# Window attention with a SwiGLU gate in float32: the split weights in six tiles of half a unit in place of three of a whole one

## The chip, the core and the metric

The kernel runs on one core of a Trainium2 chip. The metric is the device time of one launch in microseconds (us); of three runs of the kernel before, the median is 863.67 us (863.49 to 864.08). Five engines work side by side, each through its own instructions in order: TensorE (PE in the profile, PEld for its weight loads), VectorE (DVE), ScalarE (ACT), GpSimd (POOL) and SyncE (SP), which here issues nearly all of the DMA transfers. They wait for each other by semaphores.

## What is computed

```python
x = A_x                                   # 2048 tokens x 512
xn = _layernorm(x, axis=-1)
qkv = xn @ wqkv                           # 32 heads of 16
scores = einsum("bhqd,bhkd->bhqk", q, k) * (Dh ** -0.5)   # the 256 keys up to the query
s = (softmax(scores) @ v) @ wo
f = (silu(xn @ w_gate) * (xn @ w_up)) @ w_down            # 512 -> 1792 -> 512
return x + s * silu(f)
```

## The kernel before

The products with weights are made in parts: every weight and every activation is split into a high part (rounded to `float32r`) and a low part (the rest), and high times high, low times high and high times low are summed. The array of TensorE is used as two halves of 64 rows each, called half 0 and half 1 here, which work at the same time on different products; each product needs both halves, one after the other, and its PSUM bank is handed from one half to the other by a small VectorE copy (`ho`).

The tokens go in four chunks of 512. The dense work is a list of 120 **units** in an order that is fixed when the program is built: `Proj` (q and k of two groups of heads, PSUM tiles `a`), `Values` (`vp`), `GateUp` (gate `g` and up `u` of 128 hidden columns), `Down` (`d`) and `Wo` (`s`). A unit has two **items** (the last `Wo` has four), and an item fills one PSUM bank. In `Proj` and `GateUp` (class `Stationary`) item 0 reads only the first 512 columns of the unit's weights and item 1 only the second 512. In `Values`, `Down` and `Wo` (class `Moving`) the items are tokens, and each reads all of the unit's weights.

Between the dense matmuls stands the attention, in 32 units of four heads, numbered in the names: for unit 7 the products `b7_...` (for the row maxima, read by VectorE as `jk`), then `c7_...` (scores, turned into `p` by an ACT exponential, then masked by POOL), then `pv7_...`. The `b` and `c` products share four PSUM banks (`pr0` to `pr3`), so a new one can only begin when ACT or DVE has read an old one.

**Weights.** Unit j's weights are fetched by one SP DMA into a raw tile `wr` of 128x1024 (two such buffers, one more for j = 2). The split is two ACT copies that make `wh` (line 413) and two POOL subtractions that make `wl` (line 418), 512 columns each. `wh` and `wl` are tiles of 128x1024 in three buffers each, so unit j takes those of unit j-3. `w_split` (line 399) queues the four instructions when the raw tile has landed and unit j-3 has wholly ended (`item_end`, line 441), and the fetch of unit j+2 is queued half a microsecond ahead of the end of both low halves (line 426). A unit's first item may start when all of its weights are split (line 1360).

**Order.** All of this is laid out when the program is built: a planner keeps a model of each engine's clock, and from it decides which half takes which matmul next (`choice`, `next_mm`), and in which order ACT, POOL, DVE and SP get their instructions (`do`, `dma`, `pump`: among those ready the one with the smallest ready time plus slack). What comes out is one fixed list per engine; on the chip each engine works through its list and waits by semaphores where it has to. So a change of the planner's rules changes all of the lists. Each of SP's DMAs takes one of eight semaphores in turn, and so can only be issued when the one eight issues ahead of it has landed.

Of the kernel before, what the change touches and what calls it, by code (L numbers as in the profile page):

```python
# [10 lines left out]
F32R = mybir.dt.float32r  # L11
BF16 = mybir.dt.bfloat16
AF = mybir.ActivationFunctionType
ALU = mybir.AluOpType
# [3 lines left out]
P = 128  # L18
# [6 lines left out]
KC = D // P  # L25
# [29 lines left out]
def tile_window_attention_swiglu_gate(  # L55
# [10 lines left out]
    nc = tc.nc  # L66
    ctx.enter_context(tc.manual_schedule())
    pers = ctx.enter_context(tc.tile_pool(name="pers", bufs=1))
# [14 lines left out]
    def sb(name, shape, dtype, kind, n):  # L83
        return pers.tile(shape, dtype, name=name, tag=ring(kind, n), bufs=1)

    def f32(ap):
        return ap.bitcast(F32)
# [18 lines left out]
    def do(e, ready, cost, fn, then=None, slack=0.5, can=None, lat=None):  # L106
        seq[0] += 1
        queue[e].append((ready + slack, seq[0], ready, cost, fn, then, can, LAT.get(e, 0.0) if lat is None else lat))
# [16 lines left out]
    def timer(t, fn, *a):  # L125
        seq[0] += 1
        heapq.heappush(timers, (t, seq[0], fn, a))
# [41 lines left out]
    fb_free = {f"pf{i}": 0.0 for i in range(NF)}  # L169
    rb_free = {f"pr{i}": 0.0 for i in range(NR)}  # L170

    def bank_time(pool, n=1):
        t = sorted(v for v in pool.values() if v is not None)
        return t[n - 1] if len(t) >= n else None
# [49 lines left out]
    normed = {}  # L224
# [85 lines left out]
    xhigh = {}  # L310
    xlow = {}
# [42 lines left out]
    def half(r):  # L354
        return slice(R * r, R * r + R)

    def latest(times):
        times = list(times)
        return None if any(t is None for t in times) else max(times)

    class Unit:
        src = None
        width = 0

        def wts(self, r):
            return wtile[self.n]


        def inputs(self, i):
            return 0.0  # L370

    wtile = {}
    wready = {}
    landed = {}
    ended_unit = {}

    def w_fetch(j):
        u = weighted.get(j)
# [16 lines left out]

    raw = {}
    wpart = {}

    def w_split(j):
        if j not in landed or (j >= 3 and j - 3 not in ended_unit):  # L400
            return
        t = max(landed.pop(j), ended_unit.get(j - 3, 0.0))
        w = weighted[j].width
        hi, lo = [], []
        cuts = [(a, min(a + 512, w)) for a in range(0, w, 512)]
        left = [len(cuts)]

        def high(a, b):
            if not hi:
                hi.append(sb(f"wh{j}", [P, 1024], F32R, "wh", 3))  # L410
                lo.append(sb(f"wl{j}", [P, 1024], F32R, "wl", 3))
                wtile[j] = [hi[0], lo[0]]
            nc.scalar.activation(hi[0][:, a:b], raw[j][:, a:b], AF.Copy)  # L413

        def low(a, b):
            if j == 0 and a == 0:
                nc.gpsimd.tensor_copy(spare, xt[0, list(normed)[-1][1]][:, :1])
            nc.gpsimd.tensor_tensor(lo[0][:, a:b], raw[j][:, a:b], f32(hi[0][:, a:b]), op=ALU.subtract)  # L418

        def done(t, a):  # L420
            wpart[j, a, 1] = t
            left[0] -= 1
            if left[0] == 0:
                wready[j] = t
                if j:
                    timer(t - 0.5, w_fetch, j + 2)

        def after_high(t, a, b, sl):
            wpart[j, a, 0] = t
            do("G", t, 0.17 + 0.0021 * (b - a), lambda: low(a, b), lambda t: done(t, a), sl, lambda: len(normed) >= 4)  # L430

        for n, (a, b) in enumerate(cuts):
            sl = (0.0 if j >= 3 else 0.2) + 0.3 * n
            if j == 0:
                sl = -3.0 + 0.1 * n
            do("S", t, 0.13 + 0.00078 * (b - a), lambda a=a, b=b: high(a, b),
               lambda t, a=a, b=b, sl=sl: after_high(t, a, b, sl), sl)

    item_ended = {}

    def item_end(j, t):
        item_ended[j] = item_ended.get(j, 0) + 1
        if item_ended[j] == 2 * weighted[j].items:
            ended_unit[j] = t
            w_split(j + 3)

    def handover(pb):
        nc.vector.tensor_copy(pers.tile([MW, 1], F32, name="ho", tag=ring("ho", 2), bufs=1), pb[:MW, 0:1])  # L448
# [1 line left out]
    def mm(pb, a, b, first, last):  # L450
        return nc.tensor.matmul(pb, a, b, start=first, stop=last, skip_group_check=True)  # L451
# [43 lines left out]
    class Stationary(Unit):  # L495

        width = 1024
        items = 2

        def inputs(self, i):
            if self.c == 0 and self.n == 0:
# [1 line left out]
            return latest(xready.get((self.c, k)) for k in range(KC))  # L505

        def mms(self, i, r, pb):
            w = [t.rearrange("p (a k n) -> p a k n", a=2, k=KC) for t in self.wts(r)]
            xs = xn[self.c % 2]
            if self.c == 0 and self.n == 0 and i == r:  # L510
                for a, b in ((0, 0), (1, 0), (0, 1)):
                    for part in range(2):
                        n = slice(256 * part, 256 * part + 256)
                        for k in range(KC):
                            def go(first, last, k=k, a=a, b=b, n=n):
                                return mm(pb[:, n], w[a][half(r), i, k, :], xs[b][half(r), k, n], first, last)
                            yield 256, go, lambda k=k, a=a, b=b, part=part: latest(
                                [(xlow if b else xhigh).get((k, part)), wpart.get((0, 512 * i, a))]
                            )
                return  # L520
            for k in range(KC):
                for a, b in PAIRS:
                    def go(first, last, k=k, a=a, b=b):
                        return mm(pb, w[a][half(r), i, k, :], xs[b][half(r), k, :], first, last)
                    yield 512, go

    class Proj(Stationary):
# [107 lines left out]
    class Moving(Unit):  # L635
# [2 lines left out]
        items = 2  # L638

        def mms(self, i, r, pb):  # L640
            w = [t[:, : self.width].rearrange("p (k n) -> p k n", n=256) for t in self.wts(r)]
            per = 4 // self.items
            for t in range(per):
                tok = slice((per * i + t) * P, (per * i + t + 1) * P)
                for k in range(self.width // 256):
                    for a, b in PAIRS:
                        def go(first, last, t=t, k=k, a=a, b=b, tok=tok):
                            mm(
                                pb[:, t * 256 : t * 256 + 256], self.act(k, a)[half(r), tok],
                                w[b][half(r), k, :], first, last,  # L650
                            )
                        yield 256, go

# [626 lines left out]
    weighted = {}  # L1280
# [30 lines left out]
    def next_mm(r):  # L1311
        if extra[r]:
            cols, go, then = extra[r].pop(0)
            go()
            issue(r, cols)
            if then:
                then(clock[r] + 0.25)
            return
        if run[r] is None:
            n, opens = choice(r)  # L1320
            u, i = stream[n]
            if opens:
                opened[0] += 1
                banks[n], tags[n] = bank(fb_free, u.name(i))
                if isinstance(u, Wo):
                    u.begin(i)
            else:
                half_done[r].remove(n)
            run[r] = [list(u.mms(i, r, banks[n])), 0, n, opens]
        todo, m, n, opens = run[r]  # L1330
        u, i = stream[n]
        cols, go = todo[m][:2]
        go(opens and m == 0, not opens and m == len(todo) - 1)
        issue(r, cols)
        if r == 0:
            work[0] += cols * MM / 512
        run[r][1] += 1
        if run[r][1] < len(todo):
            return
        run[r] = None  # L1340
        t = clock[r] + 0.2
        item_end(u.n, t)
        if opens:
            pb = banks[n]
            half_done[1 - r].append(n)
            do("V", t, 0.1, lambda: handover(pb), lambda t: handed.__setitem__(n, t), -1.0)
        else:
            closed[0] += 1
            tag = tags.pop(n)
            u.done(i, banks.pop(n), t, lambda t: fb_free.__setitem__(tag, t))  # L1350

    def choice(r):
        t = max(clock[r], now[0])
        for n in half_done[r]:
            if handed.get(n, 1e9) <= t:
                return n, False
        n = opened[0]
        if n < len(stream):
            u, i = stream[n]
            w = wpart.get((0, 512 * i, 0)) if u.n == 0 else wready.get(u.n)  # L1360
            w = latest([bank_time(fb_free), u.inputs(i), w])
            if w is not None and w <= t:
                return n, True
        return None
# [28 lines left out]
    while True:  # L1393
        now[0] = max(front[0], min(clock))
        while marks and marks[-1][0] <= work[0] / PACE - LEAD:
            _, fn, a = marks.pop()
# [11 lines left out]
        done = False  # L1408
        if not any(extra):
            s = work[0] / PACE - LEAD  # L1410
            for st in sorted(streams, key=lambda st: st[-1][0] if st else 1e9):
                if not st:
                    continue
                due, need, fn, a = st[-1]
# [4 lines left out]
                t = need(*a)  # L1419
                if t is not None and t <= now[0]:  # L1420
# [4 lines left out]
                    done = True  # L1425
# [4 lines left out]
        if able:  # L1430
            idle = 0
            r = min(able, key=lambda r: clock[r])
# [45 lines left out]
```

## Time and profile before

| | |
|---|---|
| median of 3 runs | 863.67 us |
| the profiled execution, its own time | 865.33 us |
| span of its trace | 863.6 us |
| PE matmuls busy | 854.2 us (99%) |
| POOL, ACT, DVE busy | 595.9, 495.7, 486.2 us |
| the 240 ACT copies `wh` | 136.4 us, 616 ns mean |
| the 240 POOL subtractions `wl` | 296.7 us, 1259 ns mean |
| HBM read and written | 107.74 and 29.62 MB, 159 GB/s over the span |

Times in the views are counted from the start of the span. A row of the timeline gives start, duration, engine, line, operation, output<-inputs, shape and count, and in brackets the idle time of the engine ahead of it with what ended it. A row of SP is the issue of a DMA, not its transfer. Matmuls are pipelined: their starts say more than their durations, whose ends are modelled.

### The profile page before, as it was taken

The page shows a single profiled execution, that of the slowest core. Times are in us where ns is not written, and L with a number is a line of the kernel's source. Part 1 is how long each engine was busy: PE and PEld are TensorE (multiplying, and loading weights), DVE is VectorE, ACT ScalarE, POOL GpSimd, SP SyncE. Part 2 cuts the span into 40 slices and gives each one's busy share as a digit, 9 for nine tenths or more (in the row PEclk, how much of TensorE's full clock was granted, in tenths as well). Part 3 has the DMA queues.
Part 4 walks back from the last instruction along what each step waited for, and adds up shares of the span by engine and source line. Part 5 has one row for each costly group of instructions (what it writes and reads, how often), then busy time and mean ns, then how long its engine had stood idle before and what let it go on. Part 6 is the DMA issues. An engine that isn't in the chain of part 4 may idle for free.

```text
span 863.6 us, 29615 instructions
## 1 busy us (share of the span) xinstructions
PE 854.2 (99%) x11960; PEld 785.1 (91%) x11960; DVE 486.2 (56%) x1633; ACT 495.7 (57%) x1056; POOL 595.9 (69%) x630
## 2 busy tenths in 40 slices
PE   9999999999999999999999999999999999999997
PEld 8999999899799898999799999999999989889897
DVE  4364566555566555656565656566556656645234
ACT  4355555546665566565677566655656665656532
POOL 7555566658776775666879586666668697869764
PEclk9999999999999999999999999999999999999999
DMA  5764645455756963464777866455556668553241
GB/s 176 198 179 132 195 112 172 142 156 153 195 154 183 275 171 111 96 181 123 174 201 185 223 183 192 108 174 136 165 135 174 176 188 223 166 147 113 87 149 62
DMA packets 67628, 139.58 MB, mean 162 GB/s; under 512 B 12690, under 2 KB 21394, under 8 KB 67492
## 3 DMA queue, kind: packets, MB, share of 16 engines
q1 hardware_dynamic: 67204, 137.17, 57.3%
q8 instruction: 94, 1.54, 0.8%
q10 hardware_dynamic: 288, 0.52, 0.2%
q14 instruction: 42, 0.34, 0.2%
HBM read 107.74 MB, written 29.62 MB: 159 GB/s over the span
## 4 chain that ended last, share of the span: by engine, by line
PE 94%; DMA 3%; DVE 1%; ACT 1%; issue 0%; SPq 0%; POOL 0%; DVEq 0%; POOLq 0%; ACTq 0%
PE u L451 18%; PE d L451 18%; PE g L451 18%; PE a L451 11%; PE pv L1152 8%; PE c L1115 5%; PE s L451 5%; PE vp L451 5%; PE b L961 5%; DMA r<-rd 1%; DMA wr<-wgu 1%; DVE jk L969 0%; DMA xt<-x 0%; PE xp L469 0%; ACT wh L413 0%
## 5 line engine op out<-in xcount | busy, mean ns | idle before, releaser
L418 POOL TENSOR_TENSOR wl<-wr,wh 128x512 fp32r<-128x512 f32 x240 | 296.7, 1259 | 166.0 <-ACT wh L413 146.9
L969 DVE CUSTOM_DVE_ANT_0 jk<-b,maskb 128x384 bf16<-128x384 f32 (+2 forms) x512 | 271.7, 531 | 152.1 <-PE b L961 87.4
L1076 ACT ACTIVATE p<-c 128x384 f32<-128x384 f32 (+1 forms) x480 | 206.8, 496 | 87.1 <-PE c L1115 78.5
L451 PE MATMUL d<-wh,hh 64*128 64x256 f32 x1792 | 236.7, 278 | 0.0
L451 PEld LDWEIGHTS d<-wh,hh 64*128 64x128 f32 x1792 | 208.7, 185 | 1.4 <-issue 0.8
L451 PE MATMUL d<-wl,hh 64*128 64x256 f32 x896 | 191.7, 279 | 0.0
L413 ACT ACTIVATE wh<-wr 128x512 fp32r<-128x512 f32 x240 | 136.4, 616 | 69.1 <-issue 15.6
L451 PE MATMUL g<-xh,wh 64*128 64x512 f32 x448 | 173.3, 395 | 0.0
L451 PE MATMUL g<-xl,wh 64*128 64x512 f32 x448 | 172.9, 395 | 0.0
L451 PE MATMUL g<-xh,wl 64*128 64x512 f32 x448 | 172.6, 394 | 0.0
L451 PE MATMUL u<-xh,wh 64*128 64x512 f32 x448 | 172.2, 395 | 0.0
L451 PE MATMUL u<-xl,wh 64*128 64x512 f32 x448 | 171.6, 395 | 0.0
L451 PE MATMUL u<-xh,wl 64*128 64x512 f32 x448 | 171.4, 395 | 0.0
L451 PEld LDWEIGHTS d<-wl,hh 64*128 64x128 f32 x896 | 143.1, 185 | 0.4
L961 PE MATMUL b<-k,q 48*128 48x384 f32 (+1 forms) x512 | 113.3, 339 | 2.0 <-ACT p L1076 2.0
L1089 POOL TENSOR_SCALAR_AFFINE_SELECT p<-p 128x512 f32<-128x512 f32 x128 | 81.1, 637 | 48.9 <-ACT p L1076 44.3
L1115 PE MATMUL c<-q,k 49*128 49x384 f32 (+1 forms) x704 | 106.2, 305 | 0.7 <-ACT p L1076 0.7
L451 PE MATMUL a<-xh,wh 64*128 64x512 f32 (+1 forms) x264 | 88.6, 396 | 0.2 <-DVE ho L448 0.2
L451 PE MATMUL a<-xl,wh 64*128 64x512 f32 (+1 forms) x264 | 87.5, 387 | 0.0
L451 PE MATMUL a<-xh,wl 64*128 64x512 f32 (+1 forms) x264 | 86.8, 386 | 0.0
L451 PEld LDWEIGHTS g<-xh,wl 64*128 64x128 f32 x448 | 82.3, 186 | 3.0
L451 PEld LDWEIGHTS g<-xl,wh 64*128 64x128 f32 x448 | 82.0, 185 | 3.1 <-issue 0.2
(102 smaller groups left out, 2039.6 us busy)
## 6 DMA issues: line engine op xcount, KB each, us to landing
wr<-wgu SPq DMA_DIRECT2D x56, 512.0 KB
k<-qkd SPq DMA_DIRECT2D x48, 192.0 KB
wr<-wqk SPq DMA_DIRECT2D x16, 512.0 KB
qkd<-qkh SPq DMA_DIRECT2D x32, 256.0 KB
qkd<-qkl SPq DMA_DIRECT2D x32, 256.0 KB
q<-qkd SPq DMA_DIRECT2D x64, 128.0 KB
wr<-wdn SPq DMA_DIRECT2D x16, 512.0 KB
od<-ev SPq DMA_DIRECT2D x32, 256.0 KB
```

The source lines that it names most:

```text
L413: nc.scalar.activation(hi[0][:, a:b], raw[j][:, a:b], AF.Copy)
L418: nc.gpsimd.tensor_tensor(lo[0][:, a:b], raw[j][:, a:b], f32(hi[0][:, a:b]), op=ALU.subtract)
L451: return nc.tensor.matmul(pb, a, b, start=first, stop=last, skip_group_check=True)
L961: nc.tensor.matmul(pb[:, :w], qs[u % 3][r : r + 48, p, qb * P : (qb + 1) * P], ks[u % 3][r : r + 48, p, lo : lo + w], start=True, stop=True,)
L969: nc.vector.tensor_tensor_reduce(junk[:, :n], pb[:, :n], maskb[:, 3 * P - n :], 1.0, -3.0e38, ALU.add, ALU.max, m[:, col : col + 1],)
L1076: nc.scalar.activation(t[:, h, :], pc[:, a:b], AF.Exp, scale=DH ** -0.5)
L1089: nc.gpsimd.affine_select(s, s, [[0, 4], [1, P]], ALU.is_ge, 0.0, base=0, channel_multiplier=-1)
L1115: nc.tensor.matmul(pc[:, at0 : at0 + w], ks[u % 3][r : r + 49, p, k0 : k0 + P], qs[u % 3][r : r + 49, p, qb * P : qb * P + w], start=(i == ...
L1152: nc.tensor.matmul(pbs[r][0][32 * j : 32 * j + 32, q0:q1], vt[half(r), (4 * c + kb) % VT, VW * (4 * g + j) : VW * (4 * g + j) + 32], t[hal ...
```

## The change

`wh` and `wl` become tiles of 128x512, six tags each, of which half a of unit j takes number (2j + a) mod 6: the same memory, the same buffers, in halves. Each half has its own conditions: it is split when the raw tile has landed and the same half of unit j-3 is free (`w_cut`), and a half is free when all items that read it have ended on both halves of the array (`uses`: item a alone for `Stationary`, all items for `Moving`; `item_end`). An item of a `Stationary` unit needs only its own half to start (`need`); a `Moving` one needs both. The fetch of unit j+2 is still queued when both low halves are done. The numbers of instructions, their shapes and the bytes moved stay.

```diff
-        def wts(self, r):
-            return wtile[self.n]
+        def wts(self, a):
+            return wtile[self.n, a]
+        def uses(self, a):
+            return range(self.items)
+        def need(self, i):
+            return latest(wready.get((self.n, a)) for a in range(2))
...
     def w_split(j):
-        if j not in landed or (j >= 3 and j - 3 not in ended_unit):
+        for a in range(2):
+            w_cut(j, a)
+
+    def w_cut(j, a):
+        old = divmod(2 * j + a - NW, 2)
+        if j not in landed or (j, a) in wtile or (old[0] >= 0 and old not in wfreed):
             return
-        t = max(landed.pop(j), ended_unit.get(j - 3, 0.0))
...
-                hi.append(sb(f"wh{j}", [P, 1024], F32R, "wh", 3))
-                lo.append(sb(f"wl{j}", [P, 1024], F32R, "wl", 3))
+        wtile[j, a] = [
+            pers.tile([P, 512], F32R, name=f"w{s}{j}_{a}", tag=f"w{s}{(2 * j + a) % NW}", bufs=1) for s in "hl"
+        ]
...
+        def done(t):
+            wready[j, a] = t
+            if j and (j, 1 - a) in wready:
+                timer(t - 0.5, w_fetch, j + 2)
...
+        t = max(landed[j], wfreed.get(old, 0.0))
+        do("S", t, 0.13 + 0.00078 * m, lambda: nc.scalar.activation(hi, raw[j][:, n], AF.Copy), after_high, sl)
...
-    def item_end(j, t):
-        item_ended[j] = item_ended.get(j, 0) + 1
-        if item_ended[j] == 2 * weighted[j].items:
-            ended_unit[j] = t
-            w_split(j + 3)
+    def item_end(n, t):
+        j, i = n
+        u = weighted[j]
+        item_ended[n] = item_ended.get(n, 0) + 1
+        for a in range(2):
+            if (j, a) not in wfreed and all(item_ended.get((j, i)) == 2 for i in u.uses(a)):
+                wfreed[j, a] = t
+                w_cut(*divmod(2 * j + a + NW, 2))
...
     class Stationary(Unit):
+        def uses(self, a):
+            return (a,)
+        def need(self, i):
+            return wpart.get((0, i)) if self.n == 0 else wready.get((self.n, i))
...
-            w = wpart.get((0, 512 * i, 0)) if u.n == 0 else wready.get(u.n)
-            w = latest([bank_time(fb_free), u.inputs(i), w])
+            w = latest([bank_time(fb_free), u.inputs(i), u.need(i)])
```

The planner makes other lists of this. Two places are shown, both at the start of a chunk's turn in the attention. In the names the number after the underscore at the end is a buffer's number and says nothing.

SP's list where the weights of units 32 and 33 are fetched, before:

```order
L94 DMA qkd_65<-qkl1_2_3935 8x16x512
L94 DMA qkd_65<-qkh1_3_3973 8x16x512
L94 DMA od_66<-ev6_3961 128x512
L94 DMA qkd_65<-qkl1_3_3974 8x16x512
L94 DMA wr32_4050<-wgu 128x1024
L94 DMA wr33_4113<-wgu 128x1024
L94 DMA q0_72<-qkd_65 32x2x512
```

and in the changed program:

```order
L94 DMA qkd_65<-qkl1_2_3953 8x16x512
L94 DMA od_66<-ev6_4026 128x512
L94 DMA wr32_4081<-wgu 128x1024
L94 DMA qkd_65<-qkh1_3_4110 8x16x512
L94 DMA wr33_4142<-wgu 128x1024
L94 DMA qkd_65<-qkl1_3_4111 8x16x512
L94 DMA q0_72<-qkd_65 32x2x512
```

The fetch of `wr32` has moved ahead of two stores of q and k (`qkd<-qkh1_3`, `qkd<-qkl1_3`), and `wr33` ahead of one of them.

ACT's list at the same place, where unit 32's weights are split, before:

```order
L1076 ACTIVATE p_88<-c7_0_2_4153 128x384
L1076 ACTIVATE p_88<-c7_0_3_4154 128x384
L1076 ACTIVATE p_88<-c7_1_0_4170 128x384
L1076 ACTIVATE p_88<-c7_1_1_4171 128x384
L1076 ACTIVATE p_88<-c7_1_2_4199 128x384
L1076 ACTIVATE p_88<-c7_1_3_4200 128x384
L413 ACTIVATE wh32_4230<-wr32_4050 128x512 x2
L1076 ACTIVATE p_88<-c7_2_0_4239 128x384
```

and in the changed program:

```order
L1084 ACTIVATE p_88<-c7_0_3_4202 128x384
L1084 ACTIVATE p_88<-c7_0_2_4201 128x384
L438 ACTIVATE wh32_0_4148<-wr32_4081 128x512
L1084 ACTIVATE p_88<-c7_1_1_4224 128x384
L438 ACTIVATE wh32_1_4150<-wr32_4081 128x512
L1084 ACTIVATE p_88<-c7_1_0_4223 128x384
L1084 ACTIVATE p_88<-c7_1_2_4283 128x384
L1084 ACTIVATE p_88<-c7_1_3_4284 128x384
```

The first half of unit 32's split stands four exponentials earlier than before, the second three.

SP's list one chunk later, before:

```order
L94 DMA r1_0_8010<-rd_67 128x1x512
L94 DMA o1_1_8036<-od_66 128x1x512
L94 DMA r1_1_8037<-rd_67 128x1x512
L94 DMA wr59_8054<-wv 128x1024
L94 DMA wr60_8078<-wdn 128x768
```

and in the changed program:

```order
L94 DMA r1_0_8129<-rd_67 128x1x512
L94 DMA o1_1_8153<-od_66 128x1x512
L94 DMA wr59_8164<-wv 128x1024
L94 DMA r1_1_8154<-rd_67 128x1x512
L94 DMA wr60_8195<-wdn 128x768
```

The fetch of `wr59` has moved ahead of the load `r1_1<-rd`. On ACT the first half of unit 59's split moves ahead by four instructions (before `p<-c15_2_3` instead of behind `oh1_1`).

More of the change, by code (lines that the diff above doesn't have):

```diff
@@ L374, in tile_window_attention_swiglu_gate @@
     landed = {}
-    ended_unit = {}
     def w_fetch(j):
@@ L397, in tile_window_attention_swiglu_gate @@
     wpart = {}
+    wfreed = {}
+    NW = 6
     def w_split(j):
-        if j not in landed or (j >= 3 and j - 3 not in ended_unit):
-            return
-        t = max(landed.pop(j), ended_unit.get(j - 3, 0.0))
[L403 to L409, printed above, removed]
-                hi.append(sb(f"wh{j}", [P, 1024], F32R, "wh", 3))
-                lo.append(sb(f"wl{j}", [P, 1024], F32R, "wl", 3))
-                wtile[j] = [hi[0], lo[0]]
-            nc.scalar.activation(hi[0][:, a:b], raw[j][:, a:b], AF.Copy)
@@ L415, in low @@
-        def low(a, b):
+        for a in range(2):
[3 more added lines that the diff above has]
+        if j not in landed or (j, a) in wtile or (old[0] >= 0 and old not in wfreed):
+            return
+        n = slice(512 * a, min(512 * a + 512, weighted[j].width))
+        m = n.stop - n.start
+        wtile[j, a] = [
+            pers.tile([P, 512], F32R, name=f"w{s}{j}_{a}", tag=f"w{s}{(2 * j + a) % NW}", bufs=1) for s in "hl"
+        ]
+        hi, lo = (t[:, :m] for t in wtile[j, a])
+        sl = (0.0 if j >= 3 else 0.2) + 0.3 * a
+        if j == 0:
+            sl = -3.0 + 0.1 * a
+        def low():
@@ L416, in low @@
             if j == 0 and a == 0:
                 nc.gpsimd.tensor_copy(spare, xt[0, list(normed)[-1][1]][:, :1])
[L418 to L437, printed above, removed]
-    item_ended = {}
-    def item_end(j, t):
-        item_ended[j] = item_ended.get(j, 0) + 1
-        if item_ended[j] == 2 * weighted[j].items:
-            ended_unit[j] = t
-            w_split(j + 3)
+            nc.gpsimd.tensor_tensor(lo, raw[j][:, n], f32(hi), op=ALU.subtract)
@@ new lines, in done, with after_high @@
+        def done(t):
+            wready[j, a] = t
+            if j and (j, 1 - a) in wready:
+                timer(t - 0.5, w_fetch, j + 2)
+        def after_high(t):
+            wpart[j, a] = t
+            do("G", t, 0.17 + 0.0021 * m, low, done, sl, lambda: len(normed) >= 4)
+        t = max(landed[j], wfreed.get(old, 0.0))
+        do("S", t, 0.13 + 0.00078 * m, lambda: nc.scalar.activation(hi, raw[j][:, n], AF.Copy), after_high, sl)
+    item_ended = {}
+    def item_end(n, t):
[6 more added lines that the diff above has]
+                w_cut(*divmod(2 * j + a + NW, 2))
@@ L507, in mms @@
         def mms(self, i, r, pb):
-            w = [t.rearrange("p (a k n) -> p a k n", a=2, k=KC) for t in self.wts(r)]
+            w = [t.rearrange("p (k n) -> p k n", k=KC) for t in self.wts(i)]
             xs = xn[self.c % 2]
@@ L515, in go @@
                             def go(first, last, k=k, a=a, b=b, n=n):
-                                return mm(pb[:, n], w[a][half(r), i, k, :], xs[b][half(r), k, n], first, last)
+                                return mm(pb[:, n], w[a][half(r), k, :], xs[b][half(r), k, n], first, last)
                             yield 256, go, lambda k=k, a=a, b=b, part=part: latest(
-                                [(xlow if b else xhigh).get((k, part)), wpart.get((0, 512 * i, a))]
+                                [(xlow if b else xhigh).get((k, part)), (wready if a else wpart).get((0, i))]
                             )
@@ L523, in go @@
                     def go(first, last, k=k, a=a, b=b):
-                        return mm(pb, w[a][half(r), i, k, :], xs[b][half(r), k, :], first, last)
+                        return mm(pb, w[a][half(r), k, :], xs[b][half(r), k, :], first, last)
                     yield 512, go
@@ L640, in mms @@
         def mms(self, i, r, pb):
-            w = [t[:, : self.width].rearrange("p (k n) -> p k n", n=256) for t in self.wts(r)]
+            w = [[t.rearrange("p (k n) -> p k n", n=256) for t in self.wts(a)] for a in range(2)]
             per = 4 // self.items
@@ L649, in go @@
                                 pb[:, t * 256 : t * 256 + 256], self.act(k, a)[half(r), tok],
-                                w[b][half(r), k, :], first, last,
+                                w[k // 2][b][half(r), k % 2, :], first, last,
                             )
@@ L1341, in next_mm @@
         t = clock[r] + 0.2
-        item_end(u.n, t)
+        item_end((u.n, i), t)
         if opens:
```

## The prediction

> **What bounds the kernel now.** I read the page's busy times first, then the waits of PE, then the timelines of PE, ACT and SP at the few places where PE stood.
>
> ```profile
> span 863.6 us, 29615 instructions
> PE 854.2 (99%) x11960; PEld 785.1 (91%) x11960; DVE 486.2 (56%) x1633; ACT 495.7 (57%) x1056; POOL 595.9 (69%) x630
> ...
> PE b L961 <- ACT p L1076: 2.0, 2, 1.3
> PE warm L235 <- DVE warm L230: 1.1, 1, 1.1
> PE xp L340 <- ACT xt L270: 0.7, 1, 0.7
> PE c L1115 <- ACT p L1076: 0.7, 1, 0.7
> PE a L451 <- DVE ho L448: 0.2, 1, 0.2
> ```
>
> PE is the bound, and in all the waits of its whole list there is none for `wh` or `wl`: the weights are ready when they are wanted. What the change loosens was not waited for directly. All that it can move is the two kinds of PE time that are left: the stalls on ACT's exponentials `p`, and the time in which one half of the array has no matmul while the other works, which the busy time doesn't show.
>
> The pace of one half comes from two successive rows of g (half 0) with u (half 1) between them: 18.50 less 18.27 is 0.23 us for 512 columns.
>
> ```profile
> 18.27 0.39 PE L451 MATMUL g<-xh,wh 64*128 64x512 f32 x1
> 18.34 0.39 PE L451 MATMUL u<-xh,wh 64*128 64x512 f32 x1
> 18.50 0.40 PE L451 MATMUL g<-xl,wh 64*128 64x512 f32 x1
> ```
>
> With it the stalls can be measured from start to start:
>
> ```profile
> 225.91 0.33 PE L961 MATMUL b<-k,q 48*128 48x384 f32 x1
> 227.56 0.44 PE L961 MATMUL b<-k,q 48*128 48x384 f32 x1 [1.31 <-ACT p L1076]
> ...
> 229.18 0.39 PE L451 MATMUL g<-xl,wh 64*128 64x512 f32 x1
> 230.23 0.44 PE L961 MATMUL b<-k,q 48*128 48x384 f32 x2 [0.66 <-ACT p L1076]
> ...
> 425.45 0.39 PE L451 MATMUL u<-xh,wl 64*128 64x512 f32 x1
> 426.52 0.44 PE L1115 MATMUL c<-q,k 49*128 49x384 f32 x2 [0.68 <-ACT p L1076]
> ```
>
> 1.65 less 0.18 (384 columns) is 1.47, 1.05 less 0.23 is 0.82, and 1.07 less 0.23 is 0.84. So **place 1** (225 to 230) costs 2.3 us and **place 2** (425) 0.84. Why the exponentials were late stands in ACT's list:
>
> ```profile
> 225.98 1.15 ACT L413 ACTIVATE wh<-wr 128x512 fp32r<-128x512 f32 x2 [1.70 <-DMA wr<-wgu]
> 227.04 0.85 ACT L1076 ACTIVATE p<-c 128x384 f32<-128x384 f32 x2
> ...
> 425.10 0.61 ACT L413 ACTIVATE wh<-wr 128x512 fp32r<-128x512 f32 x1
> 425.62 0.85 ACT L1076 ACTIVATE p<-c 128x384 f32<-128x384 f32 x2
> ```
>
> At place 1 ACT stood 1.70 us at the split of unit 32, whose weights hadn't landed, with two exponentials behind it that free the bank which PE wanted. The weights stop PE after all, through ACT's list. SP shows when they landed, since it can't issue before the transfer eight issues earlier is there:
>
> ```profile
> 213.71 1.94 SPq L94 DMA_DIRECT2D qkd<-qkl  x1
> 215.74 2.66 SPq L94 DMA_DIRECT2D wr<-wgu  x2
> ...
> 222.60 0.30 SPq L94 DMA_DIRECT2D q<-qkd  x1
> ...
> 225.97 0.30 SPq L94 DMA_DIRECT2D k<-qkd  x1
> ...
> 228.56 0.30 SPq L94 DMA_DIRECT2D k<-qkd  x1
> ```
>
> Eight issues back these are the last q/k store (landed 222.6), `wr32` (225.97) and `wr33` (228.56): in the order of issue, and 3.4 and 2.6 us apart.
>
> **The change, part by part.**
>
> *Instructions.* 240 copies, 240 subtractions and 120 fetches of the same shapes remain. At the rows' means nothing is added or taken:
>
> ```profile
> L418 POOL TENSOR_TENSOR wl<-wr,wh 128x512 fp32r<-128x512 f32 x240 | 296.7, 1259 | 166.0 <-ACT wh L413 146.9 <-PE g L451 5.8 <-PE b L961 4.9
> L413 ACT ACTIVATE wh<-wr 128x512 fp32r<-128x512 f32 x240 | 136.4, 616 | 69.1 <-issue 15.6 <-PE u L451 10.5 <-PE d L451 9.8
> ```
>
> ACT and POOL get more waits for semaphores, since each half has its own. Both idle over 30% of the span, which hides it: 0. Earlier starts of a unit are worth nothing by themselves either, as no PE wait names `wh` or `wl`.
>
> *PE's list.* Both programs give each half of the array the same matmuls; only the turns differ. Priced at the pace above, with a matmul starting when the one ahead of it in the list has started and its own half is free, the halves wait for their turn 24.7 and 25.0 us in the list of before and 23.8 and 24.6 in the other; the half that ends last ends 0.9 us earlier. The largest such stretch of before is
>
> ```profile
> 211.82 2.67 PE d L451 x31
> ```
>
> where for some 1.7 us one unit of `Down` had half 1 alone; in the changed list a `Proj` stands beside it there. The changed list has a stretch of 2.1 us elsewhere, at the start of unit 9's scores. Net: **-0.9 us**, with ends of 0 (what is late next takes it) and -1.5 (the lead that holds for most of the list).
>
> *Place 1.* Two things move (both are in the lists shown above): `wr32` goes ahead of two stores, and its split ahead of three or four exponentials. The first helps, the second harms. When does `wr32` land? Its issue waits for POOL's `wl` of unit 30:
>
> ```profile
> 213.10 4.49 POOL L418 TENSOR_TENSOR wl<-wr,wh 128x512 fp32r<-128x512 f32 x4 [0.25 <-ACT wh L413]
> ```
>
> Here POOL idled 0.25 us for `wh30`, which now stands ahead of `qkh1_3` on ACT, so the issue comes 0.25 earlier. The two stores of 256 KB no longer lie ahead. By bytes each is half a fetch, 1.3 to 1.7 us; by rows moved (the lists show 8x16 rows against 128) it is as much as a fetch, 2.6 to 3.4. Two of them: 2.6 to 6.8; I take 4.5, near the middle, as no row is nearer to one end. `wr32` then lands at 225.97 - 0.25 - 4.5 = 221.2.
>
> ACT needs from there 0.58 for the first half, 0.43 for an exponential, and the same again: done at 222.2 and 223.2. PE wants these two banks at `c7_1_2` and `b8_0_2`:
>
> ```profile
> 223.03 0.34 PE L1115 MATMUL c<-q,k 49*128 49x384 f32 x1
> ...
> 224.04 0.33 PE L961 MATMUL b<-k,q 48*128 48x384 f32 x1
> ```
>
> The new list has them 1.6 and 1.9 us earlier, at 221.4 and 222.1. The stall is 0.8 and, 222.9 against 223.2, another 0.3: 1.1 in place of 2.3, **-1.2 us**. `wr33` still has one store ahead of it less, so lands about 226.0; its two copies and two exponentials end at 228.0, and PE wants that bank at 231.9 - 2.3 - 2.2 + 1.1 = 228.5. No second stall. The ends: at 218.9 no stall (-2.3), at 223.1 a stall of 3.0 (+0.7).
>
> ```profile
> 231.91 0.34 PE L961 MATMUL b<-k,q 48*128 48x384 f32 x1
> ```
>
> The Trainium skill (DMA: Bandwidth & Descriptors, "Why a DMA increments its semaphore by 16 and not by 1") says that a transfer is spread over the largest number of engines, up to 16, that divides the slowest dimension of both sides. By it a store with 8 outer rows runs on 8 engines and lasts as long as a fetch of twice its bytes, which is the upper end above: the stall would go wholly, and the sum would be 1.1 us lower. The spacing of 3.4 and 2.6 us can't tell, since both are fetches.
>
> *Place 2.* `wr59` goes ahead of `r1_1<-rd`, and its split ahead of four instructions.
>
> ```profile
> 411.84 11.26 DMA r<-rd
> ...
> 423.12 0.30 SPq L94 DMA_DIRECT2D q<-qkd  x1
> 424.74 2.05 SPq L94 DMA_DIRECT2D k<-qkd  x2
> ```
>
> `r1_1` landed at 423.1 and `wr59` at 424.7, 1.6 later, again in order. Ahead of `r1_1`, `wr59` lands before 423.1; how long before, the rows bound only by `r1_1`'s own time, 1.6 (by the spacing behind it) to some 4.7 (as two stores above). At 420.0 to 423.1 ACT, which comes to that split at about 421.2, stands 0 to 1.9 us, with some 2 us until PE wants the next bank. The exponentials that were late at 425.6 then have no split with late weights ahead of them, and the stall goes: **-0.84 us**, with 0 as the other end.
>
> *New stalls.* Nearly all first halves are split earlier in ACT's list than before, by up to 7 us, and many now stand close behind their landing; a fetch that is late blocks ACT as at place 1. But the fetches move ahead too, as they hang on the same halves, and PE's four banks cover a microsecond. Ends: 0, and two more places like place 2 (1.7). I take **+0.4**.
>
> *Sum*: -0.9 - 1.2 - 0.84 + 0.4 = **-2.5 us**. The profiled execution took 865.33 us, its span and 1.7 around it, and would take 862.8; it lies 1.7 above the median of the runs, to which the difference applies: 863.67 - 2.5 = **861.1 us**.
>
> **The rivals.**
>
> *Only the turns count* (862.8): the stalls on `p` keep their size, because ACT merely waits for the same landings at another place in its list. For it: both splits stand nearer to their landing than before. Against it: both fetches are issued ahead of what delayed them.
>
> *Nothing moves* (863.7): PE is 99% busy and doesn't wait for weights, and the turns gained are lost to whatever is late next.
>
> *The landing stays and the split is early: slower.* If `wr32` lands at 225.97 in spite of its new place, ACT stands with four exponentials behind it instead of none of them: done at 227.0 and 228.0 against 221.4 and 222.1, a stall of 5.9 in place of 2.3, +3.6. The same at place 2, `wr59` at 424.7 with PE wanting `c15_2_2`'s bank at about 423.5 and getting it at 426.8: 3.3 in place of 0.84, +2.5. With -0.9 and +0.4: +5.6, **869.3 us**. Place 1 turns from gain to loss where `wr32` lands after 222.4. The Trainium skill speaks for this one: the same page, "Queues, rings and completion order", says that completion is not first in, first out for an issuing engine. By that rule an earlier issue needn't land earlier; the five landings read above came in order.
>
> **How the numbers follow.** What can be told from no change is about 0.2%, 1.7 us: faster is below 861.9, slower above 865.4. The forecast has 0.55, nearly all of it faster (0.48, the rest within). Only the turns: 0.22, a third of it faster. Nothing moves: 0.08. The early split: 0.15, from 865 where one place goes wrong to 869.3 where both do. That makes 0.55 faster, 0.31 the same, 0.14 slower. The range: the forecast's lower ends together (-1.5, -2.3, -0.84, 0) give 859.0; upward it takes in the rivals up to one place gone wrong, 865.0.
>
> **What would show it.** In the changed profile: PE's waits on `p` under 1.5 us in all against 2.7; the stall near 225 down to about one, with ACT's idle before `wh32` short and SP's issue eight behind `wr32` released near 221; no wait of PE near 425; no chain through `wr<-wgu` there. It is wrong if ACT's idle before `wh` with DMA as its end grows past the 1.70 seen here, if PE shows waits on `p` at new places of over a microsecond, or if unpaired stretches of PE turn up that the two lists don't have.

## The result, and the profile after

The changed kernel takes 859.1 us (median of 6 runs, 857.99 to 861.66) against 864.08 for the kernel before beside it (863.49 to 864.92): a ratio of 0.9944 [0.9929, 0.9959], 4.8 us less, where 2.5 were forecast. The time lies in the range, 0.1 us above its lower end of 859.0. The profiled execution took 858.88 us with a span of 857.2, against 865.33 and 863.6.

From the page of the changed kernel, busy times, and the two rows that the waits of PE over the whole span hold (us in total, times, longest):

```profile
span 857.2 us, 29679 instructions
PE 851.1 (99%) x11960; PEld 792.0 (92%) x11960; DVE 485.9 (57%) x1633; ACT 495.9 (58%) x1056; POOL 597.3 (70%) x630
...
PE warm L235 <- DVE warm L230: 1.1, 1, 1.1
PE g L455 <- issue: 0.5, 1, 0.5
```

The waits on the exponentials `p`, 2.0 and 0.7 us before, are gone from both places, and no row has come in their stead but one of 0.5 us at 380, for which the trace shows no releaser. The work of ACT and POOL is the same within 1.4 us.

The timeline of SP where `wr32` is fetched, and ACT's where it is split:

```profile
209.48 0.33 SPq L94 DMA_DIRECT2D od<-ev  x1
211.19 0.34 SPq L94 DMA_DIRECT2D wr<-wgu  x1
212.65 0.58 SPq L94 DMA_DIRECT2D qkd<-qkh  x1
213.69 0.33 SPq L94 DMA_DIRECT2D wr<-wgu  x1
214.89 0.58 SPq L94 DMA_DIRECT2D qkd<-qkl  x1
```

```profile
217.44 0.85 ACT L1084 ACTIVATE p<-c 128x384 f32<-128x384 f32 x2
218.18 0.63 ACT L438 ACTIVATE wh<-wr 128x512 fp32r<-128x512 f32 x1
218.70 0.49 ACT L1084 ACTIVATE p<-c 128x384 f32<-128x384 f32 x1
219.07 0.64 ACT L438 ACTIVATE wh<-wr 128x512 fp32r<-128x512 f32 x1
```

ACT comes to the first half at 218.18 and doesn't stand there (1.70 us before). By the trace's semaphore events (the last update that a transfer makes), from which all landings behind the prediction are taken, `wr32` had landed at 214.86: 3.7 us behind its issue, where it had been 10.2.

But PE was ahead before it came to this place. The first product of `pv6`, in the timelines of PE, before and in the changed kernel:

```profile
208.54 1.71 PE L1152 MATMUL pv<-p,v 64*32 64x320 f32 x49
```

```profile
205.91 1.93 PE L1160 MATMUL pv<-p,v 64*32 64x320 f32 x64
```

(The first row's count ends with its window.) 2.6 us of the 6.4 between the two spans are won ahead of 209, where neither place 1 nor place 2 has been reached; 1.1 of them are there at the first `pv0` (69.5 in place of 70.6). This is no chance of one execution: `pv6` starts between 208.48 and 208.76 in all seven traces with PE's list of before, and between 205.91 and 206.02 in all three with the changed list. The laying out of PE's lists had 0.9 at this product.

### The profile page after: what moved, and what is told of

Read it like the earlier page. It is cut to its first block, busy times and chain, and to the rows that moved or that the text cites. A ratio compares the mean times of both kernels' runs of the same rounds, so it can differ in the third digit from the quotient of the medians.

```text
span 857.2 us, 29679 instructions
## 1 busy us (share of the span) xinstructions
PE 851.1 (99%) x11960; PEld 792.0 (92%) x11960; DVE 485.9 (57%) x1633; ACT 495.9 (58%) x1056; POOL 597.3 (70%) x630
## 4 chain that ended last, share of the span: by engine, by line
PE 97%; DMA 1%; DVE 1%; issue 0%; ACT 0%; SPq 0%; DVEq 0%; ACTq 0%
PE g L455 19%; PE u L455 18%; PE d L455 18%; PE a L455 11%; PE pv L1160 8%; PE c L1123 6%; PE s L455 5%; PE vp L455 5%; PE b L969 5%; PE warm L235 1%; DMA wr<-wdn 1%; PE xp L473 0%; DVE jk L977 0%; PE xp L340 0%; PE mt L1003 0%
## 5 line engine op out<-in xcount | busy, mean ns | idle before, releaser
L438 ACT ACTIVATE wh<-wr 128x512 fp32r<-128x512 f32 x240 | 142.6, 620 | 81.6 <-PE u L455 24.7
L455 PE MATMUL a<-xh,wh 64*128 64x512 f32 (+1 forms) x264 | 90.4, 395 | 0.0
L455 PE MATMUL a<-xh,wl 64*128 64x512 f32 (+1 forms) x264 | 88.6, 386 | 0.0
L455 PEld LDWEIGHTS g<-xh,wh 64*128 64x128 f32 x448 | 82.7, 186 | 2.6 <-issue 0.2
```

The lines of the kernel that those rows point to most:

```text
L438: do("S", t, 0.13 + 0.00078 * m, lambda: nc.scalar.activation(hi, raw[j][:, n], AF.Copy), after_high, sl)
```

## The experiments

Three questions were open: whether the order of SP's transfers by itself makes the two stalls, what the store's shape has to do with it, and where the rest of the gain comes from. Ratios are to the kernel before, run on the same chip.

### SP's order alone, in the kernel before

Each tag's transfer is held back until the one named has been issued; b_sp1 has the first two of the three pairs, b_sp2 the third, b_sp12 all. All other engines keep their lists. Shown is `emit`; its two empty tables and the places where it is put around the issues are left out.

```diff
+    DEFER = {'qkh1_3': 'wr32', 'qkl1_3': 'wr33', 'r1_1': 'wr59'}
+    def emit(tag, fn):
+        if DEFER.get(tag, tag) not in sent and tag in DEFER:
+            kept.setdefault(DEFER[tag], []).append((tag, fn))
+            return
+        fn()
+        sent.add(tag)
+        for t, f in kept.pop(tag, []):
+            emit(t, f)
```

> The kernel before, with SP's list alone changed at place 1: wr32 is issued ahead of both q/k stores (qkh1_3, qkl1_3) and wr33 ahead of the second, as in the changed program. All other engines keep their lists. Theory (the fetch was late because of the stores ahead of it, and its lateness stopped PE through ACT): wr32 lands 4 to 6 us earlier than 225.97, ACT's idle ahead of wh32 (1.70) goes, the stall of 2.3 us on the exponentials at 225 to 230 goes, and the time falls by 2.0 to 2.4 us, to about 861.7. Rival (the order of issue doesn't matter, the gain comes from PE's new list or from the earlier splits): wr32 lands within 1 us of before and the time stays at 864.

Measured: 0.9969 [0.9955, 0.9982], median 862.38. `wr32` landed at 219.73, 6.2 us earlier and 4.6 behind its issue. ACT's timeline:

```profile
223.50 0.87 ACT L1089 ACTIVATE p<-c 128x384 f32<-128x384 f32 x2 [0.49 <-PE c L1128]
224.26 1.15 ACT L426 ACTIVATE wh<-wr 128x512 fp32r<-128x512 f32 x2
225.30 0.87 ACT L1089 ACTIVATE p<-c 128x384 f32<-128x384 f32 x2
```

No idle ahead of the split, and no row for `p` in PE's waits. The stall of place 1 came from the two stores ahead of the fetch: with their order alone changed it is gone.

> The kernel before, with SP's list alone changed at place 2: wr59 is issued ahead of the load r1_1. Theory: wr59 lands by about 421 in place of 424.7, the stall of 0.84 us at 425 goes unless the later r1_1 makes a new one, and the time falls by 0.6 to 0.9 us, to about 863.3. Rival: the load r1_1, now behind, lands 2 to 3 us later and stops oh1_1 and all behind it on ACT: the stall stays at 0.8 or grows, time 864 or more.

Measured: 1.0004 [0.9989, 1.002], no gain. `wr59` landed at 422.1, but ACT now stands at the instruction ahead of its split, which needs `r1_1`:

```profile
421.63 0.87 ACT L1089 ACTIVATE p<-c 128x384 f32<-128x384 f32 x2
425.33 0.63 ACT L907 ACTIVATE oh<-o 128x512 fp32r<-128x512 f32 x1 [2.83 <-POOL o L897]
425.87 0.61 ACT L426 ACTIVATE wh<-wr 128x512 fp32r<-128x512 f32 x1
426.39 0.85 ACT L1089 ACTIVATE p<-c 128x384 f32<-128x384 f32 x2
```

PE waits 2.0 us for the exponential behind them, by the row of its waits:

```profile
PE c L1128 <- ACT p L1089: 2.0, 1, 2.0
```

The rival was right here: which of two late transfers goes first matters only together with the order in which ACT uses them.

> Both edits of SP's list together in the kernel before. Theory: the two gains add up to 2.6 to 3.3 us, about 861.0, and PE's waits on the exponentials (2.7 us in the kernel before) nearly vanish. What the changed kernel gained beyond this (4.9 in all) would then come from the lists of the other engines. Rival (only the new PE list counts): 864.

Measured: 0.9994 [0.9981, 1.0007], median 863.67, which is 1.3 us above b_sp1; the gains don't add. Place 1's stall is gone, and 0.8 us of PE's waits, at place 2, are of the new kind (ACT idle 1.61 us ahead of `oh`).

### How regular the stalls are

The kernel before was profiled again, unchanged.

> The kernel before once more, to see how much its stalls vary from one execution to the next. At place 1 the stall was 2.6 us beyond the best of five runs with this PE list, and 1.9 in the run with SP's list changed at place 2 alone. At place 2 it was 0.9 here and nothing in two runs whose lists agree there. If both stalls belong to the lists, they show again at 1.9 to 2.6 and about 0.9. If place 2 was a chance of that execution, it is below 0.3 and r1_1 lands some 2 us earlier against PE's work.

Measured: 863.34 us, span 861.6, which is 2.0 less than in the first profile. PE's waits on the exponentials:

```profile
PE b L961 <- ACT p L1076: 0.7, 2, 0.4
```

Both are at place 1. Measured by how far PE's starts fall back there behind its list, laid out at its pace, the stalls come to 1.3 us (2.6 in the first profile, where the prediction read 2.3 from two gaps); `wr32` landed at 225.2 and ACT stood 0.68 us in place of 1.70. At place 2 there is none: `r1_1` landed at 420.6, where it had been 423.1. Nor do b_sp1 and a_both (below), whose lists agree there with those of before, show a wait on `p` at place 2. So place 1 is regular, with a size that varies by over a microsecond, and place 2 was a chance of the execution on which the prediction was made.

### Half tiles with whole conditions

```diff
         def uses(self, a):
-            return (a,)
+            return range(self.items)
         def need(self, i):
-            return wpart.get((0, i)) if self.n == 0 else wready.get((self.n, i))
+            return wpart.get((0, i)) if self.n == 0 else latest(wready.get((self.n, a)) for a in range(2))
```

> The changed kernel with the six half tiles, but an item of a Stationary unit again needs both halves and frees them only with the whole unit. The planner then gives PE exactly the list of before. Theory (the time is won by the order of the fetches and the new lists, not by the halves themselves): the stall near 225 is back at 1.9 to 2.6 us and the time is that of before, 863.5 to 865. Rival (separate tiles have waits of their own for each half, and that is what saves): the time is near the changed kernel's, 859 to 861.

Measured: 0.9997 [0.9988, 1.0006]; the stall near 225 is there (0.93 and 0.76 us by the same measure, together a little less than the 1.9 expected at least). The lists of all engines, SP's too, are here those of before. Separate tiles win nothing by themselves. All of the gain comes from the lists that the finer conditions let the planner make.

### The changed kernel with SP's order put back

With the same `emit`:

```diff
+    DEFER = {'wr32': 'qkl1_3', 'wr33': 'qkl1_3', 'wr59': 'r1_1'}
```

> The changed kernel, with SP's list alone put back at both places: wr32 and wr33 behind both q/k stores, wr59 behind the load r1_1. Theory (earlier fetches pay at place 1 only; the rest of the gain is PE's new list and what else moved): wr32 lands at 219 to 221 in place of 214.9, ACT stands 0.5 to 2.5 us at its first half, PE 0 to 1.5, wr59 lands near 416.5 without a stall, and the time is 859.5 to 860.5. Rival (the split stands early, so a fetch that is late costs more than before): stalls of 3 us and more, time 862 or more.

Measured: 1.0036 [1.0023, 1.005], median 867.01: 0.9% above the changed kernel (1.0036/0.9944), and above the kernel before. My theory expected 859.5 to 860.5 and missed; the rival named it. ACT's timeline at place 1:

```profile
217.56 0.85 ACT L1097 ACTIVATE p<-c 128x384 f32<-128x384 f32 x2
224.10 0.63 ACT L451 ACTIVATE wh<-wr 128x512 fp32r<-128x512 f32 x1 [5.68 <-DMA wr<-wgu]
224.63 0.47 ACT L1097 ACTIVATE p<-c 128x384 f32<-128x384 f32 x1
225.00 0.62 ACT L451 ACTIVATE wh<-wr 128x512 fp32r<-128x512 f32 x1
225.53 1.24 ACT L1097 ACTIVATE p<-c 128x384 f32<-128x384 f32 x3
```

And PE's waits:

```profile
PE c L1136 <- ACT p L1097: 6.4, 2, 5.1
PE g L468 <- issue: 2.1, 1, 2.1
```

`wr32` lands at 224.07, 9.2 us later than in the changed kernel, and ACT, which now comes to the split at 218.4 with four exponentials close behind it, stands 5.68 us. The loss is the slower rival of the prediction, at its place and by its mechanism; its stall at place 1 was priced at 5.9 us (in place of 2.3, so 3.6 more than before), and is some 7 (PE's starts lose 5.9, 0.7 and 0.6 there). Place 2 costs 1.6. The wait of 2.1 us at 292 has no releaser in the trace, and what it is stays open. All these sizes are those of the profiled execution, whose 869.76 us are 2.8 above the median.

### The shape of the stores

The lists are those of before; only the destination rows of the 64 q/k stores change. The rows of q and k are then permuted, so this form doesn't compute the attention.

```diff
-                    qkd[g, :, :, :, (1 - s) * DH : (2 - s) * DH, c * TC : (c + 1) * TC]
-                    .rearrange("a p h d n -> (a p h) d n"), tiles[s],
+                    qkd[g, s, :, :, :, c * TC : (c + 1) * TC].rearrange("p h d n -> (p h d) n"), tiles[s],
```

> The kernel before with every list unchanged; the q/k stores write 128 rows of 512 (of the same buffer, to other rows, so that q and k hold permuted rows and the output is not the attention's) in place of 8 blocks of 16 rows. Same bytes. If a store's time goes by its bytes: wr32 lands where it did (225.97 within 0.5), stall 2.3, time 864. If it goes by the rows of its outer dimension, the two stores ahead of wr32 take half as long: wr32 lands 2.5 to 3.5 us earlier, the stall falls to 0.5 or less, the time by 1.5 to 2.3 us.

Measured: 0.9968 [0.9956, 0.998], median 862.07. The two stores landed 2.6 and 3.7 us behind their issue in place of 5.5 and 8.9, `wr32` at 219.9, 4.8 behind its issue in place of 10.2. PE's waits hold none on `p`:

```profile
PE warm L235 <- DVE warm L230: 1.1, 1, 1.1
PE a L451 <- DVE ho L448: 0.2, 1, 0.2
```

Over all 64 stores the median from issue to landing fell from 5.8 to 4.1 us. With the same bytes, the same 128 rows and the same order the stall is gone. So neither bytes nor rows moved, from which the prediction took its two bounds, settle the time of a store here: its outer rows count, and the two stores ahead of `wr32` came near the upper bound of 6.8 us (5.7 in b_sp1).

The traces also show a difference in how the stores are carried out. Each store raises its semaphore 9 times in the kernel before and 16 times here. And the row of the queue (packets, MB, share of time), before and then in b_rows, has 512 packets more for the same MB, 8 for each store:

```profile
q1 hardware_dynamic: 67204, 137.17, 57.3%
```

```profile
q1 hardware_dynamic: 67716, 137.17, 58.3%
```

This agrees with the rule of the Trainium skill (DMA: Bandwidth & Descriptors, "Why a DMA increments its semaphore by 16 and not by 1") by which 8 outer rows get 8 engines. The loads `o`, `r` and `den` also raise their semaphores 9 times, the late `r1_1` among them; another shape for them wasn't tried.

A form that computes the whole attention gets there by the order of the weights' columns: with d outside, a store is 16 blocks of 8 rows. On the changed kernel:

```diff
-    wqk = np.concatenate([q, k], axis=3).reshape(KC, P, NG // 2, 2, P)
+    wqk = np.concatenate([q, k], axis=3).reshape(KC, P, NG, 8, DH).swapaxes(3, 4)
+    wqk = wqk.reshape(KC, P, NG // 2, 2, P)
...
-                    .rearrange("a p h d n -> (a p h) d n"), tiles[s],
+                    .rearrange("a p h d n -> d (a p h) n"), tiles[s],
```

> The changed kernel with every list the same, and the columns of the q/k weights in another order, so that a store of q or k is 16 blocks of 8 rows in place of 8 blocks of 16: same bytes, same rows in the end. If a store's time goes by its outer dimension (8 against 128 made the two stores ahead of wr32 land 2.9 and 5.4 us earlier in the kernel before), stores land 1.5 to 2.5 us earlier than in the changed kernel. There is no stall on them left to remove, so the time is that of the changed kernel within 0.7 us: 858.4 to 859.4. If stores by blocks of 8 rows aren't quicker, landings stay as they were and the time too.

Measured: 0.9927 [0.9915, 0.9939], median 857.8, the fastest of all here, in another measurement than the changed kernel's 859.1 (0.9944), whose interval overlaps. Over all 64 stores the median from issue to landing is 3.7 us, where the changed kernel has 5.4: within the expected 1.5 to 2.5. At place 1 there is less to see: `qkl1_3` lands 1.5 us earlier (220.3 against 221.8), `qkh1_3` only 0.1, and `wr32` at 216.9 in place of 214.9, though its issue is only 0.1 later. The time lies 0.6 below the expected 858.4 to 859.4, and the 1.3 us between the medians isn't traced to the stores: of the 1.1 us between the two spans 0.8 are lost at 380, where the row of 0.5 us isn't there in this run.

### Other lists, with quick stores

With quick stores no list has a wait on `p`, so what is compared is the lists. That of before stands there in the form with 128 rows, the others with 16 blocks. The edits: one of the two conditions of the change taken back (`need` or `uses`, as shown for a_both), or in the kernel before

```diff
-        dma(now[0], go, then, slack=1.0, kb=512 if j > 2 else 400)
+        dma(now[0], go, then, slack=1.1, kb=512 if j > 2 else 400)
```

and the same with 0.5.

> The changed kernel with stores of 16 blocks (the version that took 857.8), but an item of a Stationary unit again needs both halves to start; halves are still freed one by one. With quick stores the kernel with PE's list of before took 862.1, the one with the changed list 857.8: the lists differ by 4.3 us, of which my laying out of the lists had priced 0.9. This list ends 0.6 later than that of before by the same laying out. Theory (finer conditions give the planner a freer choice and so a denser list): between the two, 859 to 861. Rival (every nudge of the planner draws another list, and before to after was one draw): anywhere from 858 to 864, 862 or more being as likely as not.

> As the last, with the other part taken back: an item needs only its own half, and a unit's halves are freed together. The list ends 2.3 us later than that of before by my laying out. Theory of the freer choice: between 858 and 862. By the laying out with the offsets of the two known lists: 861.0 to 864.4. Rival of the draw: 858 to 865.

> The kernel before with stores of 16 blocks, and a nudge that means nothing: the slack of the weight fetches is 1.1 in place of 1.0. PE's list agrees with that of before up to about 280 us and is another behind it, ending 1.8 us later by my laying out. Theory of the freer choice: a nudge alone gives nothing, 862 to 864. Rival of the draw: 859 to 865, with 860 or less speaking for it clearly.

> The same with the slack at 0.5: the fetches go ahead of other transfers in the planner's order, as the change made them go, without half tiles. PE's list agrees with that of before up to about 415 us and ends 0.3 us later by my laying out. Theory of the freer choice: 861.5 to 863. Rival of the draw: 859 to 865. If it falls to 859 or less, fetches that go earlier are enough, and half tiles aren't needed.

In the table "end" is the end of PE's list laid out at the pace of 0.233 us for 512 columns, as for the prediction's -0.9:

| kernel, all with quick stores | end by the laying out | span | median | ratio |
|---|---|---|---|---|
| the changed list (a_d16) | 811.6 | 856.1 | 857.8 | 0.9927 |
| the list of before (b_rows) | 812.5 | 860.0 | 862.07 | 0.9968 |
| before, slack 0.5 | 812.8 | 859.8 | 861.88 | 0.9968 [0.9956, 0.9979] |
| changed, both halves needed | 813.1 | 859.9 | 861.92 | 0.9968 [0.9957, 0.998] |
| before, slack 1.1 | 814.3 | 860.6 | 862.31 | 0.9968 [0.9955, 0.998] |
| changed, halves freed together | 814.8 | 862.2 | 864.0 | 0.9996 [0.9988, 1.0005] |

Either condition alone wins nothing over the list of before, so the expectation of the freer choice (each between the two) failed for both. The nudged lists stand within 0.3 us of the list of before, which speaks against the draw: neither reached 860. Of these lists only the one with both conditions is denser. But it is one list; a nudged version of the changed planner wasn't tried, and that the next one would be as dense isn't shown.

The laying out puts the lists very nearly in the order of their times, but shows too little of the differences: 3.2 us between the first and the last, where the spans differ by 6.1.

## Why the prediction was right, and where its sizes were off

**PE's list: the term that was mis-sized.** Forecast -0.9, with -1.5 as its far end. With the stalls out of both, the changed list takes 3.9 us less than that of before (spans 860.0 and 856.1; by the ratios 0.41% or 3.5 us, on two chips). The first `pv6` shows the same ahead of both places, in the kernel with quick stores and the list of before, and in a_d16:

```profile
208.52 1.93 PE L1151 MATMUL pv<-p,v 64*32 64x320 f32 x64
```

```profile
206.00 1.93 PE L1160 MATMUL pv<-p,v 64*32 64x320 f32 x64
```

The step that failed was to price the lists by the turns of the halves alone. Laid against the measured starts behind 14 us, what PE loses beyond the laying out is 34.9 us with the list of before and 32.1 with the changed one. Of the 2.8 between them 1.8 stand at matmuls that carry a wait for a semaphore (4.3 against 2.5), 0.6 at `pv` (22.0 against 21.4), the rest elsewhere. This split is an estimate, which depends on how the laying out prices each matmul. If these are waits they are short ones, as the view of PE's waits shows only one of 0.2 us of them (b_rows); for what each waits wasn't sorted out, so why this list is denser stays open. The windows show as little: PE counts as busy for 50.00 of 50 us from 100 to 150 and from 150 to 200 in either kernel.

**Place 1: right in mechanism, more in size.** Forecast -1.2, between -2.3 and +0.7. The stall went wholly. Two parts of the landing were off. The issue came at 211.19, 4.3 us earlier than the 215.5 worked out, because POOL came to `wl30` at 209.16 in place of 213.10: its two `oh` subtractions, ahead of it in the list, now ran at 203.4 in place of 209 and 211.6. And the way from issue to landing fell from 10.2 to 3.7 us, where the two stores had been priced at 4.5 together; in b_sp1 it fell by 5.7, in b_rows by 5.4. But what went isn't 2.3 us in every execution: 2.6 in the first profile, 1.3 in the second.

**Place 2: wrong as a term.** Forecast -0.84. The stall was a chance of one execution, absent in b_again; and the edit which the prediction credited (fetch ahead of `r1_1`) gives a stall of 2.0 us (b_sp2) or 0.8 us (b_sp12) where ACT keeps its list. In the changed kernel it does no harm, as ACT's split there stands ahead of `p<-c15_2_3` and `r1_1` is back at 416.5, 4.8 us ahead of its `oh`.

**New stalls: none.** +0.4 was taken; the waits have one of 0.5 us, with no releaser in the trace, and a_d16 doesn't show it.

**The sum.** Between the two first profiles the spans differ by 6.4: 2.6 at `pv6`, 2.6 at place 1, 0.9 at place 2, 0.3 behind. Against the second profile of before it is 4.4: 2.9 at `pv6`, 1.3, 0, 0.2. The median's 4.8 lies between. So about half of the gain or more is PE's list, which had been the smaller part of the forecast; both parts point the way that was forecast. That the time lies within the range, by 0.1 us, is luck in part: PE's list gained more than its far end of -1.5 allowed, while place 2 had nothing to give in the second profile and place 1 only 1.3.

**The slower rival** (the landing stays and the split is early) had a chance of 0.15. Its mechanism is real: with the fetches where they had been, the changed lists lose 3 us to the kernel before. In the changed kernel the fetch had moved with the split: the planner hangs both on the same halves.

## What to carry to other kernels

An engine that works through its list in order and waits for a load also holds back what is queued behind it: look for the stalls of the bound engine in the list of the engine that it waits for, and there for the transfer, and for what stands ahead of that in the queue. When a split moves ahead in such a list, its fetch must move with it: the early splits without the early fetches cost 8 us here (a_undo12 against the changed kernel), while the early fetches alone gained 0.3% (b_sp1). Profile the kernel twice before pricing a stall of under a microsecond, and don't price a reordered list by its long waits alone.

## What was not expected of the hardware

With stores of 8 outer rows, two q/k stores cost more ahead of the fetches than behind them. In the order store, store, `wr32`, `wr33` (before) the four landed at 218.0, 222.6, 226.0 and 228.6; in the order `wr32`, store, `wr33`, store with the same lists elsewhere (b_sp1) at 219.7, 221.4, 224.8 and 226.0, though the first of them was issued 2.6 us later. The stores behind a fetch add 1.7 and 1.2 us there, 2.9 and 1.2 in the changed kernel. Why isn't shown.

In all fourteen traces the 248 transfers `wr`, `qkd`, `od`, `o` and `r` landed in the order of their issue, but a small transfer can pass. In the changed kernel `q1<-ms16` (8 KB) landed at 426.5, a store that was issued ahead of it at 426.8; and in every trace two to four of the 16 loads `den` (16 KB) landed ahead of a fetch that was issued before them, by up to 1.6 us.
